# A gated second layer with seven block products for eight, in passes of three d_ff tiles and two batches

## The chip, the core and the metric

One core of a Trainium2 chip. TensorE (PE) multiplies matrices, VectorE (DVE) and ScalarE (ACT) work element by element, GpSimd (POOL) helps, SyncE (SP) issues the DMAs from one queue in order. The metric is the device time of the whole kernel in microseconds; the median of three runs before is 1274.05 us (1272.81 to 1276.3).

## The reference

Attention (4 batches, 12 heads, 448 rows, 64 columns), a feed-forward layer with squared ReLU (768 to 2048 to 768) and a gated one (768 to 1536 to 768), all in float32:

```python
q_n, k_n = rmsnorm(q, g_q), rmsnorm(k, g_k)
attn = softmax(scale * q_n @ k_n.T) @ v
x = attn.transpose(0, 2, 1, 3).reshape(B * S, H * D)     # 1792 x 768
r = np.maximum(x @ w_in, 0.0)                            # d_ff 2048
x = (r * r) @ w_out
g = x @ w_gate                                           # d_ff 1536
silu = g * (1.0 / (1.0 + np.exp(-g)))
out = (silu * (x @ w_val)) @ w_out2
```

## The kernel before

All activations lie transposed: 128 features on the partitions, the 448 rows of one batch along the free axis. So d_model is six tiles (`KD`), the second layer's d_ff twelve (`FF2`). A float32 operand is kept as two halves, `hi` (rounded to the matmul's format) and `lo` (the rest), and a product is three matmuls, hi x hi, hi x lo, lo x hi (`mm3`, the matmuls themselves at L346). ScalarE makes `hi` by a cast (L240), VectorE `lo` by a subtraction. Weights come as 64-bit words and are decoded by `chunk`: one scaling on ScalarE, one cheap row (L311) and two full rows (L315, L318) on VectorE, then the split (L333).

The two feed-forward layers run in sweeps: one batch, a range of d_ff tiles. For each tile of layer 2, `products` computes the gate (6 x 3 matmuls into a PSUM bank of `h_free`), then the value (18 matmuls), `gated` and `valued` make Sigmoid, two multiplies and the split, and `out_of` adds the tile's share to the six output sums `y` (18 matmuls), two tiles behind (`BEHIND`). Six PSUM banks hold the sums, two the products. Three batches of layer 2 are swept in two halves of six d_ff tiles (`G2`); the sums of the first half go to `y2_d` in DRAM and are read back (`Partial`, L1256, added at L1263). X tiles of a sweep are loaded and split by `load_x` (L1181 to L1184) during the sweep before.

The order of the instructions is set by a planner inside the kernel: each step is a job with a rank and with its cost on each engine that may do it; `simulate` runs them against its own clock, and whichever job has the lowest rank when an engine is free is written down next. The chip then follows that order on each engine, strictly in turn. A line in a trace is often that of a helper. In names the two numbers behind `_1_6_15` and the like are layer, sweep, tile.

Of the kernel before, what the change touches and what calls it, by code (L numbers as in the profile page):

```python
# [9 lines left out]
F32 = mybir.dt.float32  # L10
# [9 lines left out]
KD = DM // 128  # L20
# [6 lines left out]
G2 = 6  # L27
# [21 lines left out]
IO_TILES = 6  # L49
W2_SLOTS = 16  # L50
BEHIND = 2
# [28 lines left out]
def attention_two_ffn_kernel(  # L80
# [199 lines left out]
    wt, placed, free = {}, {}, []  # L280

    def load_weights(items):
# [7 lines left out]
        def chunk(key, place, c, raw_at):  # L290
# [31 lines left out]
            if c == 0:  # L322
                yield lambda: place or free
                pool, hi_tag, lo_tag = placed[key] = place or free.pop(0)
                hilo[key] = tuple(
                    pool.tile([128, DM], F32R, tag=tag, name=f"{part}_{name}{f}")
                    for part, tag in (("hi", hi_tag), ("lo", lo_tag))
                )
                parts[key] = 0
# [32 lines left out]
    def tile_at(where, shape, dtype, name):  # L362
        return where[0].tile(shape, dtype, tag=where[1], name=name)
# [28 lines left out]

    def gated(pg, where, sig):
        yield settle["P"]
        yield lambda: ea_free
        sig["at"] = ea_free.pop(0)
        t = tile_at(sig["at"], [128, S], F32, f"sig_{sig['n']}")
        yield {"A": 424}, lambda e: e.activation(out=t, in_=pg, func=ACTF.Sigmoid)  # L398
        yield {"V": 535}, lambda e: e.tensor_tensor(out=t, in0=pg, in1=t, op=ALU.mult)  # L399
        h_free.append(where)  # L400
        sig["tile"] = t

    def valued(pv, where, sig):
        yield settle["P"]
        yield lambda: s_free and "tile" in sig
        s_at = s_free.pop(0)
        s = tile_at(s_at, [128, 2, S], F32R, f"s_{sig['n']}")
        t = sig["tile"]
        yield {"V": 535}, lambda e: e.tensor_tensor(out=t, in0=pv, in1=t, op=ALU.mult)  # L409
        h_free.append(where)  # L410
        yield {"A": 467, "W": 300}, lambda e: copy(e, s[:, 0, :], t)
        yield {"W": 535, "G": 1106}, lambda e: e.tensor_tensor(
            out=s[:, 1, :], in0=t, in1=as_f32(s[:, 0, :]), op=ALU.subtract
        )
        ea_free.append(sig["at"])
        ready[sig["n"]] = s, s_at
# [573 lines left out]
    def place(slot):  # L990
        return (w1 if slot < 24 else w2), f"w{slot}", f"w{slot + 1}"
# [100 lines left out]
    M1B, F1C, F2A, F2B = range(G1, M1), range(M1, FF1), range(G2), range(G2, FF2)  # L1092
# [6 lines left out]
    order2 = [LAST - 1] + list(range(LAST - 1)) + [LAST]  # L1099
    outs = [[out[bass.ts(j, 128), bass.ts(b, S)] for j in range(KD)] for b in range(B)]  # L1100
    sweeps += [(2, b, F2A, (), None, y2_d[b]) for b in order2[:-1]]
    sweeps += [(2, order2[-1], range(FF2), F2A, None, outs[order2[-1]])]
    sweeps += [(2, b, F2B, (), y2_d[b], outs[b]) for b in order2[:-1]]
    POST = 10000
    when, steps = {}, 0
    for layer, b, fs, *_ in sweeps:
        for f in fs:
            for key in (("in", f), ("out", f)) if layer == 1 else (("g", f), ("v", f), ("o2", f)):
                when.setdefault(key, POST + steps)
            steps += layer  # L1110
# [15 lines left out]
    later += [(w, f) for f in range(FF2) for w in ("g", "v", "o2")]  # L1126
# [26 lines left out]
    w2 = ctx.enter_context(tc.tile_pool(name="w2", bufs=1, side="right", reuse_waits="tile"))  # L1153
    w3 = ctx.enter_context(tc.tile_pool(name="w3", bufs=1, side="right", reuse_waits="tile"))
    xp2 = ctx.enter_context(tc.tile_pool(name="xp2", bufs=1, side="right", reuse_waits="tile"))
    raws += [(w3, f"raw{2 + i}") for i in range(RAWS2)]
# [36 lines left out]

    def release(key):
        del wt[key]
        free.append(placed.pop(key))
# [3 lines left out]
    def products():  # L1200
        behind = []
        ys = {}
        xs = x1[LAST]
        k = POST
        for i, (layer, b, fs, last_use, partial, dst) in enumerate(sweeps):
            n = f"{layer}_{i}"
            done = None
            for f in fs:
                if f == fs[X_AT if len(fs) > 6 else 1] and i + 1 < len(sweeps):
                    nxt, done = {}, []  # L1210
                    src = (x1_d if sweeps[i + 1][0] == 1 else x2_d)[sweeps[i + 1][1]]
                    spawn(load_x(src, n, x_tiles(n, i % 2 == 0, nxt), done, k), k)
                name = f"{n}_{f}"
                if i == 0 and f < 3:
                    release(("in", f))
                elif layer == 1:
# [41 lines left out]
    def written(ps, sums, j, n, dst):  # L1258
# [5 lines left out]
        else:  # L1264
# [3 lines left out]
            yield {"A": 424}, lambda e: e.copy(y, ps)  # L1268
        yield from dma(lambda e: e.dma_start(out=dst, in_=y), 128 * S * 4)
        io_free.append(at)  # L1270
# [3 lines left out]
    def out_of(name, n, layer, f, first, last, release_it, ys, sums, dst, k):  # L1274
        key = ("out" if layer == 1 else "o2", f)
        yield lambda: key in wt and name in ready
        w = wt[key]
# [4 lines left out]
        for j in OUT_ORDER:  # L1282
            yield from mm3(ys[j], w[0], w[1], bass.ts(j, 128), s[:, 0, :], s[:, 1, :], first, last)
            if last:
                spawn(written(ys[j], sums, j, n, dst[j]), k - 2)
        s_free.append(where)
        if release_it:
            release(key)

    spawn(products(), 0)  # L1290
    simulate(lambda: finished and not timers and not any(queues.values()))

# [80 lines left out]
```

## Time and profile before

| | |
|---|---|
| median of three runs | 1274.05 us |
| the profiled execution: span, first to last instruction | 1269.9 us |
| rest of the median around the span | 4.15 us |
| TensorE busy | 1250.5 us, 6642 matmuls |
| VectorE busy | 681.6 us, 1454 instructions |
| ScalarE busy | 563.6 us, 1259 instructions |
| GpSimd busy | 158.7 us |
| DMA | 151 MB, 119 GB/s in the mean |
| layer 2 (gate, value and output matmuls) | 733 to 1266 us |

The profile gives the span of the profiled execution; a time of its own around that span is not shown, so the 4.15 us are taken from the median. A group row of the trace reads: line, engine, operation, out<-in, sizes, count | busy us, mean ns of one | idle time of the engine just before, and who ended it. Matmuls overlap, so the duration of one (366 ns) is longer than the distance between two.

### The profile page before, as it was taken

Reading aid. Unit: us, or ns where it says so; the run is one execution under the profiler, and the core shown is the slowest. Engines: PE = TensorE matmul, PEld = TensorE weight load, DVE = VectorE, ACT = ScalarE, POOL = GpSimd, SP = SyncE. Lnnn points to the kernel's source line nnn. Section 1 sums busy time; section 2 is a strip of 40 time slices with the busy share of each in tenths; the row PEclk is TensorE's granted clock in tenths of the full one; section 3 lists DMA queues with packets and bytes.
Section 4 is the critical chain, followed back from the end, with each engine's and each line's share of the span. In section 5 each row is a group of like instructions: output and inputs, shape, how many; then the busy total and the mean of one; then the engine's idle time right before and its main releaser. Section 6 shows DMA issues by size and latency. Waiting matters only on the chain.

```text
span 1269.9 us, 18473 instructions
## 1 busy us (share of the span) xinstructions
PE 1250.5 (98%) x6642; PEld 1073.4 (85%) x6642; DVE 681.6 (54%) x1454; ACT 563.6 (44%) x1259; POOL 158.7 (13%) x275
## 2 busy tenths in 40 slices
PE   8989999999999999999999999999999999999998
PEld 6656667777778998999999999999999999999998
DVE  7999985665543996459233982212159612113122
ACT  6999876776764665236122541212036311211010
POOL 5454454343200000000000000000000000000000
PEclk9999999999999999999999999999999999999999
DMA  7576664343112666436234671201037300203021
GB/s 222 170 208 179 202 189 144 108 129 123 52 65 98 227 199 218 130 123 193 74 122 131 212 250 49 86 2 44 1 101 231 123 1 1 87 1 131 1 87 44
DMA packets 87309, 151.01 MB, mean 119 GB/s; under 512 B 16481, under 2 KB 66802, under 8 KB 87218
## 3 DMA queue, kind: packets, MB, share of 16 engines
q1 hardware_dynamic: 87218, 149.84, 37.1%
q8 instruction: 52, 0.85, 0.3%
q14 instruction: 39, 0.32, 0.1%
HBM read 120.75 MB, written 29.04 MB: 118 GB/s over the span
## 4 chain that ended last, share of the span: by engine, by line
PE 79%; DVE 11%; ACT 5%; DMA 3%; issue 2%; SPq 1%; POOL 0%; DVEq 0%; ACTq 0%
PE y L346 24%; PE h_v L346 14%; PE h_g L346 14%; PE h L346 9%; PE ya L346 4%; PE h_a L346 4%; PE o L938 3%; PE sc L767 3%; PE pt L898 2%; DVE sc L795 2%; ACT ring L809 2%; ACT turned_p L240 1%; DVE ring L833 1%; DVE wt_in L318 1%; DMA raw_in<-in_w_in_dram 1%
## 5 line engine op out<-in xcount | busy, mean ns | idle before, releaser
L346 PE MATMUL h_v<-x,hi_v 128*128 128x448 f32 x576 | 164.4, 366 | 0.0
L346 PE MATMUL h_g<-x,hi_g 128*128 128x448 f32 x576 | 164.4, 366 | 0.0
L346 PE MATMUL y<-s,hi_o 128*128 128x448 f32 x576 | 164.1, 366 | 0.0
L346 PE MATMUL y<-s,hi_out 128*128 128x448 f32 x552 | 157.3, 366 | 0.9 <-ACT ys L1268 0.9
L346 PE MATMUL h<-x,hi_in 128*128 128x448 f32 x516 | 147.2, 366 | 0.0
L399 DVE TENSOR_TENSOR sig<-h_g,sig 128x448 f32<-128x448 f32 x48 | 30.0, 624 | 215.1 <-ACT sig L398 215.0
L809 ACT ACTIVATE ring<-sc,m,rms 128x448 f32<-128x448 f32 x168 | 124.2, 746 | 14.4 <-DVE m L796 5.4
L398 ACT ACTIVATE sig<-h_g 128x448 f32<-128x448 f32 x48 | 26.1, 545 | 221.8 <-PE h_g L346 221.8
L346 PEld LDWEIGHTS h_v<-x,hi_v 128*128 128x128 f32 x576 | 108.1, 188 | 9.3
L346 PEld LDWEIGHTS h_g<-x,hi_g 128*128 128x128 f32 x576 | 108.2, 188 | 9.2
L346 PEld LDWEIGHTS y<-s,hi_o 128*128 128x128 f32 x576 | 108.1, 188 | 9.3
L346 PEld LDWEIGHTS y<-s,hi_out 128*128 128x128 f32 x552 | 103.4, 188 | 10.2 <-ACT ys L1268 1.7
L346 PE MATMUL h_v<-x,lo_v 128*128 128x448 f32 x288 | 105.4, 366 | 0.0
L346 PE MATMUL y<-s,lo_o 128*128 128x448 f32 x288 | 105.4, 366 | 0.0
L346 PE MATMUL h_g<-x,lo_g 128*128 128x448 f32 x288 | 105.4, 366 | 0.0
L346 PEld LDWEIGHTS h<-x,hi_in 128*128 128x128 f32 x516 | 96.8, 188 | 8.4
L795 DVE TENSOR_REDUCE sc<-sc 128x2 f32<-128x896 f32 (+1 forms) x96 | 93.8, 977 | 15.9 <-PE sc L767 14.4
L346 PE MATMUL y<-s,lo_out 128*128 128x448 f32 x276 | 100.8, 365 | 0.0
L240 ACT COPY turned_p<-pt 128x384 f32<-128x384 f32 (+2 forms) x167 | 88.4, 541 | 23.1 <-PE pt L898 22.1
L346 PE MATMUL h<-x,lo_in 128*128 128x448 f32 x258 | 94.4, 366 | 0.0
L240 ACT CAST s<-sig 128x448 fp32r<-128x448 f32 x48 | 27.2, 566 | 131.9 <-DVE sig L409 131.8
L938 PE MATMUL o<-turned_p,v 128*64 128x448 f32 x384 | 79.5, 546 | 0.6 <-DVE turned_p L242 0.5
(160 smaller groups left out, 2236.1 us busy)
## 6 DMA issues: line engine op xcount, KB each, us to landing
raw_in<-in_w_in_dram SPq DMA_DIRECT2D x32, 384.0 KB
raw_out<-in_w_out_dram SPq DMA_DIRECT2D x32, 384.0 KB
kq<-in_kq_p_dram SPq DMA_DIRECT2D x23, 480.0 KB
xr<-x2d SPq DMA_DIRECT2D x42, 224.0 KB
raw_g<-in_w_gate_dram SPq DMA_DIRECT2D x24, 384.0 KB
raw_v<-in_w_val_dram SPq DMA_DIRECT2D x24, 384.0 KB
raw_o<-in_w_out_dram SPq DMA_DIRECT2D x24, 384.0 KB
xr<-x1d SPq DMA_DIRECT2D x36, 224.0 KB
```

The lines of the kernel that those rows point to most:

```text
L240: e.copy(out, src)
L318: yield {"W": 469}, lambda e: e.scalar_tensor_tensor(out=ti, in0=ai, scalar=3, in1=ti, op0=ALU.logical_shift_left, op1=ALU.bitwise_or)
L346: return {"P": 203}, lambda e: e.matmul(ps, lhsT=w, rhs=x, start=first, stop=last), 0
L398: yield {"A": 424}, lambda e: e.activation(out=t, in_=pg, func=ACTF.Sigmoid)
L399: yield {"V": 535}, lambda e: e.tensor_tensor(out=t, in0=pg, in1=t, op=ALU.mult)
L767: e.matmul(parts[t][:, :S], lhsT=q[a][d, bass.ts(i % 4, 128)], rhs=k[c][d], start=(p == 0), stop=(p == len(passes) - 1),)
L795: e.tensor_reduce(out=top, in_=sc, axis=AX.X, op=ALU.max, negate=True)
L809: yield {"A": 704}, lambda e: e.activation(out=slot(i), in_=parts[t][:, :S], func=ACTF.Exp, bias=m[:, t:t + 1], scale=rq[:, i:i + 1], accu ...
L833: yield {"V": 130, "G": 260}, lambda e: e.tensor_copy(dst, slot(i)[:, 384:])
L898: e.transpose(ps[:, bass.ts(j + (i > 3), 128)], p[:, bass.ts(j, 128)], ident)
L938: e.matmul(o[64 * h:64 * h + 64], lhsT=v[:, 4 * h + j], rhs=turned_p[:, 4 * h + j if j < 3 else 3], start=(j == 0), stop=(j == 3),)
```

## The change

Layer 2 is computed for a pair of batches at a time, `PAIRS` (2, 0) and (1, 3). The d_model axis is cut in two halves of three tiles. For a d_ff tile the weights form a 2 x 2 block matrix, `a11` and `a12` the two halves of the gate, `a21` and `a22` those of the value; the X tiles form another, `b11`, `b21` the halves of the first batch, `b12`, `b22` those of the second. The 2 x 2 product of blocks takes seven block products (Strassen's algorithm, in Winograd's form) of 3 x 3 matmuls instead of eight. For it four sums of weight blocks (`s1` to `s4`) and four of X blocks (`t1` to `t4`) are formed in float32 on VectorE and split into halves, and the products `p1` to `p7` are added up from PSUM on VectorE (`u2`, `u4`, `g1` and so on) into gate and value of both batches. Silu is one ScalarE operation in place of Sigmoid and a multiply.

Passes: a group of three d_ff tiles for one pair, then for the other pair; the next group starts with the pair just used, so that X changes between passes 0 and 1, 2 and 3, 4 and 5, 6 and 7. A unit is one d_ff tile of one pass (63 matmuls). After the three units of a pass come its twelve output sums (`outputs`, 108 matmuls): four begin with the first two tiles and are ended when the third is ready, the other eight follow whole. The sums of a pass go to `y2_d`, and from the pair's second pass on those of the pass before are read back and added. All eight PSUM banks serve products and sums in turn. In the built program 6363 matmuls become 6147.

The weights of layer 2 are loaded by `load_second`, from the time on when all of layer 1's are loaded; their ranks begin at six below those of their first unit, those of X at two below. Eight tiles `io` (two of them lent to the products' sums) serve X loads, partial sums and results.

```diff
-G2 = 6
-IO_TILES = 6
+IO_TILES = 7
+PAIRS = ((2, 0), (1, 3))
+GROUP = 3
+PARTIALS = 4
+SPARES = 2
...
+            if i == len(sweeps) - 2:
+                x_free.extend([(xp2, f"x{j}") for j in range(4)] + [(xp, "x6"), (xp, "x7")])
+                spawn(load_pair(0), k)
...
+        yield from second_layer(k)
...
+    def gate_value(f, slots, parts, done, temps, rank):
...
+        yield lambda: "a22" in done
+        yield from halved("a22", "a22")
+        yield lambda: "a21" in done
+        yield put("a22", "a21", "a22", ALU.add)
+        yield lambda: "a11" in done
+        yield put("a21", "a11", "a21", ALU.subtract)
+        second = []
+        spawn(last_halved("s1", "a22", lambda: second), rank)
+        spawn(last_halved("s3", "a21"), rank)
+        yield from halved("a11", "a11")
+        yield put("a11", "a22", "a11", ALU.subtract)
...
+    def load_pair(n):
...
+        rank = POST + steps + sum(2 * len(fs) for _, fs in passes[:n]) - 2
...
+        for kk in range(3):
+            parts, done, slots = {}, set(), []
+            for name, h, j in (("b11", 0, kk), ("b12", 1, kk), ("b22", 1, kk + 3), ("b21", 0, kk + 3)):
+                yield lambda: io_free
+                at = io_free.pop(0)
+                parts[name] = tile_at(at, [128, S], F32, f"{name}_{n}_{kk}"), at
+                spawn(fetched(parts[name][0], pair[h], j, name, done), rank)
+            spawn(pair_tiles(n, kk, X, slots, parts, done, rank), rank)
...
+        b1, b1_at = yield from bank_tile(f"p1_{n}_{f}")
+        yield from product(b1, "a11", "b11", True, True)
+        b6, b6_at = yield from bank_tile(f"p6_{n}_{f}")
+        got = {}
+        spawn(gate_0(got, b1, b1_at, f"{n}_{f}"), k)
+        yield from product(b6, "s2", "t2", True, True)
+        spawn(sum_2(got, b6, b6_at, f"{n}_{f}"), k)
...
+        b4, b4_at = yield from bank_tile(f"p4_{n}_{f}")
+        yield from product(b4, "a22", "t4", True, True)
+        spawn(value_0(got, b4, b4_at, (n, f, 0)), k)
...
+    def silu(t):
+        return {"A": 467}, lambda e: e.activation(out=t, in_=t, func=ACTF.Silu)
...
+    def value_0(got, ps, where, key):
+        yield settle["P"]
+        yield lambda: "u3" in got
+        u2 = got["u2"][0]
+        yield plus(u2, ps, u2)
+        h_free.append(where)
+        yield from gated(got, "g0", "u2", key)
+
+    def gated(got, gate, value, key):
+        yield lambda: gate in got
+        (g, g_at), (t, t_at) = got[gate], got[value]
+        yield {"W": 535, "G": 1106}, lambda e: e.tensor_tensor(out=t, in0=g, in1=t, op=ALU.mult)
+        ea_free.append(g_at)
+        yield lambda: s_free
+        at = s_free.pop(0)
+        s = tile_at(at, [128, 2, S], F32R, "s_%d_%d_%d" % key)
+        yield from halves_of(s, t, S)
...
+        for j, h in y_order[:ahead]:
+            ys[j, h] = yield from bank_tile(f"y2_{n}_{j}_{h}")
+            yield from chain(j, h, fs[:-1])
+        for m, (j, h) in enumerate(y_order):
+            if m >= ahead:
+                ys[j, h] = yield from bank_tile(f"y2_{n}_{j}_{h}")
+            yield from chain(j, h, fs[-1:] if m < ahead else fs)
+            spawn(summed_out(n, p, j, h, ys[j, h], sums), k)
```

The first place is VectorE at the end of layer 1's last sweep, before: the rows that end with the low half of tile 15's squares, `s_1_6_15` (`wt_v5`, `lo_g5` and the like are weights of layer 2, `r` the relu).

```order
L315 SCALAR_TENSOR_TENSOR wt_v5_0_8261<-wa_v5_0_8252,wt_v5_0_8261 128x384
L311 TENSOR_SCALAR wt_g5_1_8257<-raw_g5_1_8180 128x384
L318 SCALAR_TENSOR_TENSOR wt_v5_0_8261<-wa_v5_0_8252,wt_v5_0_8261 128x384
L333 TENSOR_TENSOR lo_g5_8274<-wt_g5_0_8210,hi_g5_8273 128x384
L315 SCALAR_TENSOR_TENSOR wt_g5_1_8257<-wa_g5_1_8242,wt_g5_1_8257 128x384
L333 TENSOR_TENSOR lo_v5_8293<-wt_v5_0_8261,hi_v5_8292 128x384
L383 SCALAR_TENSOR_TENSOR r_1_6_15_8284<-h_1_6_15_8240,r_1_6_15_8284 128x448
L311 TENSOR_SCALAR wt_v5_1_8298<-raw_v5_1_8220 128x384
L387 TENSOR_TENSOR s_1_6_15_8283<-r_1_6_15_8284,s_1_6_15_8283 128x448
```

The same place now, up to the same subtraction (`a12_2`, `s2_2`, `s4_2` and `o0` are operands of layer 2's weights, `t4_0_2` one of the first pass's X):

```order
L1293 TENSOR_TENSOR a12_2_8187<-a12_2_8077,a12_2_8187 128x384
L1315 TENSOR_SCALAR o0_0_plain_8178<-raw_o0_0_8179 128x384
L1293 TENSOR_TENSOR t4_0_2_8197<-b21_0_2_8069,t4_0_2_8197 128x448
L1298 TENSOR_TENSOR a12_2_8077<-a12_2_8077,a11_2_7967 128x384
L1318 SCALAR_TENSOR_TENSOR o0_0_plain_8178<-raw_o0_0_8179,o0_0_plain_8178 128x384
L1315 TENSOR_SCALAR o0_1_plain_8189<-raw_o0_1_8190 128x384
L1321 SCALAR_TENSOR_TENSOR o0_0_plain_8178<-raw_o0_0_8179,o0_0_plain_8178 128x384
L1293 TENSOR_TENSOR s4_2_8205<-a12_2_8077,s4_2_8205 128x384
L1318 SCALAR_TENSOR_TENSOR o0_1_plain_8189<-raw_o0_1_8190,o0_1_plain_8189 128x384
L1293 TENSOR_TENSOR o0_0_8211<-o0_0_plain_8178,o0_0_8211 128x384
L1321 SCALAR_TENSOR_TENSOR o0_1_plain_8189<-raw_o0_1_8190,o0_1_plain_8189 128x384
L393 TENSOR_TENSOR s_1_6_15_8089<-r_1_6_15_8090,s_1_6_15_8089 128x448
```

Before, one row stands between relu and subtraction of tile 15; now there are thirteen, all of them layer 2's operands, and more of these lie ahead of the relu.

The second place is VectorE at the end of the third pass (number 2), from the first sum with `p7` of the last unit to the low half of that unit's value, `s_2_5_0` (`u2`, `u4` are sums on the way to the values; `t2_3_0`, `t3_3_0`, `b21_3_0`, `t4_3_0` operands of the next pass's X):

```order
L1533 TENSOR_TENSOR u2_2_5_9730<-p7_2_5_9772,u2_2_5_9730 128x448
L1293 TENSOR_TENSOR t2_3_0_9785<-b22_3_0_9683,t2_3_0_9785 128x448
L1293 TENSOR_TENSOR t3_3_0_9786<-b12_3_0_9682,t3_3_0_9786 128x448
L1533 TENSOR_TENSOR u4_2_5_9760<-p7_2_5_9772,u4_2_5_9760 128x448
L1293 TENSOR_TENSOR b21_3_0_9787<-b21_3_0_9684,b21_3_0_9787 128x448
L1533 TENSOR_TENSOR u2_2_5_9730<-p4_2_5_9792,u2_2_5_9730 128x448
L1601 TENSOR_TENSOR u4_2_5_9760<-g1_2_5_9775,u4_2_5_9760 128x448
L1298 TENSOR_TENSOR b21_3_0_9684<-b21_3_0_9684,b22_3_0_9683 128x448
L1601 TENSOR_TENSOR u2_2_5_9730<-u1_2_5_9711,u2_2_5_9730 128x448
L1293 TENSOR_TENSOR s_2_5_1_9830<-u4_2_5_9760,s_2_5_1_9830 128x448
L1293 TENSOR_TENSOR t4_3_0_9835<-b21_3_0_9684,t4_3_0_9835 128x448
L1293 TENSOR_TENSOR s_2_5_0_9843<-u2_2_5_9730,s_2_5_0_9843 128x448
```

Five of the twelve rows prepare X of the next pass; before, a value's rows stood between weights or alone.

## Rows read from the trace of the kernel before

**Rows 1.** The page: busy time, share of the span and instructions of each engine.
```profile
PE 1250.5 (98%) x6642; PEld 1073.4 (85%) x6642; DVE 681.6 (54%) x1454; ACT 563.6 (44%) x1259; POOL 158.7 (13%) x275
```
**Rows 2.** Windows: us, busy us (x instructions) of each engine, PEclk, DMA share, GB/s.
```profile
core 0: us, PE busy (x) PEld busy (x) DVE busy (x) ACT busy (x) POOL busy (x), PEclk, DMA share, GB/s
10.00:12.00 2.00, 1.86 (x25) 1.79 (x26) 1.93 (x5) 0.09 (x1) 0.93 (x1) 1.00 0.88 239
...
406.00:450.00 44.00, 44.00 (x218) 40.66 (x217) 42.29 (x95) 28.71 (x60) 0.00 (x0) 1.00 0.62 202
733.00:1266.00 533.00, 533.00 (x2615) 490.47 (x2613) 184.25 (x353) 118.36 (x231) 0.00 (x0) 1.00 0.21 71
...
1150.00:1154.00 4.00, 4.00 (x21) 3.70 (x20) 0.98 (x2) 1.54 (x3) 0.00 (x0) 1.00 0.99 323
...
1266.00:1270.00 4.00, 0.20 (x1) 0.00 (x0) 0.86 (x2) 0.00 (x0) 0.00 (x0) 0.88 0.61 225
```
**Rows 3.** Chain of waits that ended last: start, us, engine, tile, line, matmuls.
```profile
880.84 3.65 PE y L346 x18
...
1251.51 3.69 PE h_v L346 x18
```
**Rows 4.** Who waited for whom: us in total, times, longest.
```profile
ACT sig L398 <- PE h_g L346: 221.8, 42, 6.2
...
DVE sig L409 <- PE h_v L346: 90.4, 40, 2.5
```
**Rows 5.** Groups of the page: gate and value matmuls of layer 2.
```profile
L346 PE MATMUL h_v<-x,hi_v 128*128 128x448 f32 x576 | 164.4, 366 | 0.0
L346 PE MATMUL h_g<-x,hi_g 128*128 128x448 f32 x576 | 164.4, 366 | 0.0
...
L346 PE MATMUL h_v<-x,lo_v 128*128 128x448 f32 x288 | 105.4, 366 | 0.0
...
L346 PE MATMUL h_g<-x,lo_g 128*128 128x448 f32 x288 | 105.4, 366 | 0.0
```
**Rows 6.** Timeline of VectorE, 721 to 726 us: start, us, engine, line, operation.
```profile
722.00 1.16 DVE L1184 TENSOR_TENSOR x<-xr,x 128x448 fp32r<-128x448 f32 x2
723.07 0.63 DVE L387 TENSOR_TENSOR s<-r,s 128x448 fp32r<-128x448 f32 x1
...
724.54 0.56 DVE L315 SCALAR_TENSOR_TENSOR wt_g<-wa_g,wt_g 128x384 int32<-128x384 int32 x1
725.01 0.37 DVE L311 TENSOR_SCALAR wt_v<-raw_v 128x384 int32<-128x384 uint32 x1
725.28 0.56 DVE L318 SCALAR_TENSOR_TENSOR wt_g<-wa_g,wt_g 128x384 int32<-128x384 int32 x1
```
**Rows 7.** Groups of VectorE from 400 us on, shapes kept apart.
```profile
L1184 DVE TENSOR_TENSOR x<-xr,x 128x448 fp32r<-128x448 f32 x78 | 47.1, 624 | 13.2 <-ACT x L240 12.8
...
L315 DVE SCALAR_TENSOR_TENSOR wt_g<-wa_g,wt_g 128x384 int32<-128x384 int32 x24 | 13.4, 560 | 0.1
...
L311 DVE TENSOR_SCALAR wt_g<-raw_g 128x384 int32<-128x384 uint32 x24 | 8.6, 362 | 1.1 <-DMA raw_g<-in_w_gate_dram 1.1
```
**Rows 8.** Timeline, 890 to 894 us: a value's multiply, cast and subtraction.
```profile
891.87 0.62 DVE L409 TENSOR_TENSOR sig<-h_v,sig 128x448 f32<-128x448 f32 x1 [2.45 <-PE h_v L346]
...
892.53 0.57 ACT L240 CAST s<-sig 128x448 fp32r<-128x448 f32 x1 [3.77 <-DVE sig L409]
...
893.13 0.63 DVE L412 TENSOR_TENSOR s<-sig,s 128x448 fp32r<-128x448 f32 x1 [0.63 <-ACT s L240]
```
**Rows 9.** Groups of ScalarE from 400 us on.
```profile
L398 ACT ACT_TABLE_LOAD x1 | 1.3, 1283 | 0.0
```
**Rows 10.** Timeline of TensorE, 8 to 12 us.
```profile
10.14 0.99 PE L592 MATMUL rk<-rkr,pick 128*64 128x128 f32 x16 [1.07 <-ACT rkr L636]
```
**Rows 11.** Timeline of the end: the last sums and stores.
```profile
1263.20 3.66 DVE L1263 TENSOR_TENSOR yp<-y,yp 128x448 f32<-128x448 f32 x6 [6.08 <-PE y L346]
...
1263.86 3.37 SPq L1269 DMA_DIRECT2D out_dram<-yp  x6
```

More of the change, by code (lines that the diff above doesn't have):

```diff
@@ L1107, in attention_two_ffn_kernel @@
         for f in fs:
-            for key in (("in", f), ("out", f)) if layer == 1 else (("g", f), ("v", f), ("o2", f)):
+            for key in (("in", f), ("out", f)):
                 when.setdefault(key, POST + steps)
-            steps += layer
+            steps += 1
     def gains():
@@ L1272, in written, with out_of @@
             sums.load()
[L1274 to L1277, printed above, removed]
+    def out_of(name, n, f, first, last, release_it, ys, sums, dst, k):
+        yield lambda: ("out", f) in wt and name in ready
+        w = wt["out", f]
         s, where = ready.pop(name)
@@ new lines, in attention_two_ffn_kernel, with halves_of @@
+    LAST_1 = len(sweeps) - 1
+    swept = {b: next(i for i, sw in reversed(list(enumerate(sweeps))) if sw[1] == b) for b in range(B)}
+    operand, pair_x = {}, {}
+    when2 = {f: POST + steps + sum(2 * len(fs) for _, fs in passes[:i]) + 2 * passes[i][1].index(f)
+             for f in range(FF2) for i in [next(i for i, (_, fs) in enumerate(passes) if f in fs)]}
+    def halves_of(t, plain, c):
+        yield {"A": 413 if c == WC else 467, "W": 269 if c == WC else 300}, lambda e: copy(e, t[:, 0], plain)
+        yield {"W": 469 if c == WC else 535, "G": 956 if c == WC else 1106}, lambda e: e.tensor_tensor(
+            out=t[:, 1], in0=plain, in1=as_f32(t[:, 0]), op=ALU.subtract
+        )
@@ new lines, in load_pair, with fetched @@
+    def load_pair(n):
+        pair = PAIRS[passes[n][0]]
+        X = pair_x[n] = {}
+        rank = POST + steps + sum(2 * len(fs) for _, fs in passes[:n]) - 2
+        yield lambda: all((f"1_{swept[b]}", j) in stored_at for b in pair for j in range(KD))
+        def fetched(t, b, j, name, done):
+            yield from dma(lambda e: e.dma_start(out=t, in_=x2_d[b][j]), 128 * S * 4)
+            done.add(name)
+        for kk in range(3):
[6 more added lines that the diff above has]
+            spawn(pair_tiles(n, kk, X, slots, parts, done, rank), rank)
+            for _ in range(7):
+                yield lambda: x_free
+                slots.append(x_free.pop(0))
@@ new lines, in second_layer @@
+    def second_layer(k):
+        x_of = 0
+        summed_before = set()
+        for n, (p, fs) in enumerate(passes):
+            if n and passes[n - 1][0] != p:
+                x_of = n
+            last_x = n + 1 == len(passes) or passes[n + 1][0] != p
+            last_w = n % 2 == 1
+            sums = {"used": 0}
+            for f in fs:
+                if f == fs[-1]:
+                    if last_x and n + 1 < len(passes):
+                        spawn(load_pair(n + 1), k)
+                    if p in summed_before:
+                        spawn(partials(n, p, sums, k), k)
+                yield from unit(n, f, x_of, last_x and f == fs[-1], last_w, k)
+                k += 2
+            yield from outputs(n, p, fs, sums if p in summed_before else None, last_w, k)
+            summed_before.add(p)
@@ new lines, in partials, with part @@
+    def partials(n, p, sums, k):
+        def part(j, h, at):
+            y = tile_at(at, [128, S], F32, f"yp_{n}_{j}_{h}")
+            src = y2_d[PAIRS[p][h]][j]
+            yield from dma(lambda e: e.dma_start(out=y, in_=src), 128 * S * 4)
+            sums[j, h] = y, at
+        for m, (j, h) in enumerate(y_order):
+            yield lambda: io_free and m - sums["used"] < PARTIALS and (p, j, h) in y_stored
+            spawn(part(j, h, io_free.pop(0)), k)
+    y_order = [(j, h) for j in range(KD) for h in range(2)]
@@ new lines, in summed_out @@
+    def summed_out(n, p, j, h, bank, sums):
+        ps, where = bank
+        b = PAIRS[p][h]
+        last = all(q != p for q, _ in passes[n + 1:])
+        dst = outs[b][j] if last else y2_d[b][j]
+        yield settle["P"]
+        if sums is not None:
+            yield lambda: (j, h) in sums
+            y, at = sums[j, h]
+            yield {"V": 535}, lambda e: e.tensor_tensor(out=y, in0=ps, in1=y, op=ALU.add)
+            sums["used"] += 1
+        else:
+            yield lambda: io_free
+            at = io_free.pop(0)
+            y = tile_at(at, [128, S], F32, f"yw_{n}_{j}_{h}")
+            yield {"A": 424}, lambda e: e.copy(y, ps)
+        h_free.append(where)
+        yield from dma(lambda e: e.dma_start(out=dst, in_=y), 128 * S * 4)
+        y_stored.add((p, j, h))
+        io_free.append(at)
```

322 lines of the change are left out of this document (270 added, 52 removed).

## The prediction

> **What bounds the kernel now.** I read the busy times first. TensorE works 1250.5 of 1269.9 us, VectorE 681.6 [rows 1]. The windows by stage then show that the second layer, 733 to 1266 us, is TensorE without a gap: 533 of 533 us busy at granted clock 1.00, which is the upper level, 2.4 GHz, while VectorE works 184 us and the DMA engines 21% of the time [rows 2]. The chain of waits says the same. There it is one product after the other, each of 18 matmuls, and from the start of the one at 880.84 to the end of the one at 1251.51 lie 374.36 us [rows 3], which are 102 such products: 3.670 us each, 0.2039 us a matmul. Nothing but fewer matmuls shortens this stretch as long as the other engines keep up, and they do: VectorE waits 90.4 us for value products and ScalarE 221.8 us for gate products [rows 4]. Speed does not depend on how busy VectorE is either: from 406 to 450 us it is busy 42.3 of 44 us and TensorE still puts 218 matmuls into 44.0 us [rows 2].
>
> **What the change takes away.** Gate and value are 576 + 288 matmuls each, 1728 together [rows 5]. Now there are 24 units (12 d_ff tiles, 2 pairs of batches) of 7 products with 9 matmuls, 1512. The 864 of the output stay. 216 x 0.2039 = **44.0 us** less on TensorE; layer 1 and attention keep their matmuls.
>
> **What it adds on VectorE.** Counted in the order from the first eviction of layer 2 on: 467 rows of 448 columns, 228 of 384, and 56 of the cheap decode step. What one costs when rows queue up is the distance of starts, not the duration: 0.535 us (722.00 to 723.07 for two), 0.47 (724.54 to 725.01) and 0.27 (725.01 to 725.28) [rows 6], while one alone lasts 0.624, 0.560 and 0.362 [rows 7]. The sum is 467 x 0.535 + 228 x 0.469 + 56 x 0.269 = 372 us against 2376 x 0.2039 = 484 us of matmuls: 77%. At full durations it would be 291 + 128 + 20 = 439 us, 91%. So VectorE becomes busy but not the bound on average; what matters is where it is late. The X operands of a pair (21 split tiles, 12 differences) are prepared five times, and six of the eight passes read and write partial sums. POOL gets too little of it to count. ScalarE's added casts and copies are each shorter than the VectorE row that they feed (0.57 against 0.63 us for a value's cast and subtraction [rows 8]); Silu stands for Sigmoid with one less multiply, after one table load as before (1.3 us, [rows 9]), hidden under products.
>
> **Where layer 1 meets layer 2.** This is the one place where I find a wait that can't be hidden. In the last sweep of layer 1 the preparation for the first pass is ranked ahead of the last tile's squares. From r_1_6_13 to the subtraction s_1_6_15 there are now 66 VectorE rows (35 of 448, 25 of 384, 6 cheap): 35 x 0.535 + 25 x 0.469 + 6 x 0.269 = 32.1 us; before there were 35 rows, 16.0 us. VectorE cannot begin them before product h_1_6_13 has ended. TensorE, between that end and the matmul that reads s_1_6_15's low half, has 6 products (y of 11, h 14, y of 12, h 15, y of 13, y of 14) and one matmul: 22.2 us. So it stands still for 32.1 - 22.2 = 9.9 us at least, whatever the other engines do. VectorE comes about 0.6 us late to r_1_6_13, since the sums of the sweep before are ahead of it, and once waits about 1.1 us for ScalarE's casts, which stand behind the relu and square of tile 15 in its queue; the last row's own end costs 0.1. I take **12 us**, from 10 to 16: the floor is the count above, the ceiling adds two more such waits of 2 us. What is late next there is nothing: by the time TensorE is back, the operands of the first unit stand in the same queue ahead of s_1_6_15, already done.
>
> **The clock after that gap.** Before, the level falls once, after the last matmul: from 1266 to 1270 us, with 0.20 us of matmul left, the mean is 0.88 [rows 2]. A gap of 1.07 us before 10.14 us [rows 10] did not lower it, 1.00 stands there too [rows 2]. So a gap of 12 us will meet the lower level, 1.2 GHz, and the work behind it starts there. No row shows a matmul of this kernel at that level or how long the way back takes. Bounds: nothing, and at most a stretch as long as the gap done at half speed, 6 us lost. I take **2 us**, nearer to nothing because the work behind the gap is dense. The Trainium skill ("TensorE: Matmul & The Clock Gate", Part 1: The HAM clock gate) says that TensorE returns to half clock once it has idled and has to work before it is given the full one again; the row at 1266 agrees with the first half, no row here shows the second. By that rule the term is above zero, without it the sum would be 2 us smaller.
>
> **The ends of the passes.** Four of the twelve output sums begin with two of three d_ff tiles, 24 matmuls or 4.9 us, and then need the last unit's value. Its chain is an addition, a multiply, a cast and a subtraction; in the rows the last three take 891.87 to 893.76, 1.9 us, without a queue [rows 8], so 2.5 us with the addition. But operand rows stand between. At the end of the third pass, from the sum with p7 (1.83 us before p4 ends) to the subtraction of s_2_5_0, 12 rows lie, 6.4 us; 6.4 - 1.8 + 0.1 = 4.7 against 5.1 us to the matmul that reads it. It just fits, with nothing left for a DMA that is late, and three of the rows between need tiles that were just loaded. I take 0.4 us for each of eight ends, **3 us**, from 0 to 12 (1.5 each, the length of one cast and one subtraction more).
>
> **DMA.** Layer 2 moves 18 more X loads and 54 more partial loads and stores each, 126 x 0.229 = 29 MB, to the 71 GB/s x 533 us = 38 MB of before. In the worst stretch, last unit and outputs with an X change (35 us), 12 X tiles, 12 partial loads and 12 stores are 8.3 MB, 25.6 us at the 323 GB/s of 1150 to 1154 us [rows 2]. SP's one queue holds an X load behind a store whose sum must be done first; followed row by row, the operands of the next pass are ready 2 to 4 us before TensorE wants them. I cost it at nothing, cover gone at some 3 us of lateness, 0 to 4 us in all. The tail stays: six sums and stores end 3.7 us after the last matmul [rows 2, 11]; now the last sum comes alone, at most 0.5 us less.
>
> **Sum.** -44.0 + 12 + 2 + 3 + 0 = -27 us. In the profiled execution that makes the span 1243; its span lies 4.15 us under the median of 1274.05, and I leave that part as it is: **1247 us**. Its own range is 1240 (only the counted 10 us) to 1256.
>
> **Rivals.** (a) The gap at the layer change isn't there, because the two engines drift so that VectorE enters this stretch with its preparation done. Then only the pass ends stay, -44 + 3: 1233. For it speaks that VectorE has idle time one sweep earlier; against it, that the 66 rows stand in a fixed order behind h_1_6_13.
> (b) The ends of the passes and changes of X cost 2.5 us each more, because a late load at the head of VectorE's queue holds the value chain, with 0.4 us spare: 1247 + 8 x 2.5 = 1267. For it speaks the thin margin; against it, that DMA has a quarter of its time free even there.
> (c) Slower: VectorE becomes the bound of all of layer 2. Of its rows, 261 subtract a half that ScalarE has just cast. If half of them wait 0.63 us at the head of the queue, as the one at 893.13 did [rows 8], and rows then don't overlap, 439 + 82 = 521 us stand against 484 of matmuls, +37: -44 + 37 + 14 = +7, 1281. It decides from 514 us of VectorE time on, 38% above the 372 us that I counted. For it speaks that both engines wait in order; against it that TensorE's pace leaves 60 us a pass for 45 to 54 us of VectorE rows.
> (d) The change doing less than it says can't be: the matmuls are counted in the order, 6147 against 6363.
>
> **Chances.** Forecast 0.60, (a) 0.13, (b) 0.21, (c) 0.06. The time is that of the forecast; the range, 1232 to 1268, leaves out the better part of (a), (c) and the upper part of (b), together some 2 in 10. A measurement of this kernel tells 0.3% from no change, 3.8 us. Faster than 1270.2: forecast, (a) and the greater part of (b), 0.91. Same 0.04, slower 0.05.
>
> **What would show it.** Right: TensorE's first long idle time sits before a y matmul that reads s_1_6_15, ended by VectorE, 10 to 16 us long; the granted clock falls below 1.00 there and nowhere else in layer 2; windows of one pass (60.6 us of matmuls) are 60 to 62 us long; VectorE is busy 75 to 90% of them. Wrong: no such gap (a), gaps of 2 us and more before y2 matmuls or p1 at each pass end (b), or TensorE waiting for VectorE at every p product (c).

## The result and the profile after

The kernel with seven block products takes **1246.55 us** (median of four runs, 1243.29 to 1246.79) against 1273.43 us for the kernel before on the same chip (four runs, 1272.57 to 1276.3): a ratio of 0.9776, 95% interval 0.976 to 0.9792, or 26.9 us less. The forecast was 1247.

The page of the profile after, first the span and then the busy line that answers to [rows 1]:

```profile
span 1245.0 us, 18922 instructions
...
PE 1212.4 (97%) x6426; PEld 1038.3 (83%) x6426; DVE 884.9 (71%) x1825; ACT 625.8 (50%) x1382; POOL 169.1 (14%) x285
```

TensorE has 216 records less than before, all from gate and value, and works 38.1 us less; VectorE works 203.3 us more, and its share goes from 54% to 71%. The groups of TensorE (columns as in [rows 5]; the last column is idle time before the group, and who ended it) say where TensorE stands still: nowhere within layer 2.

```profile
L352 PE MATMUL y<-s,o 128*128 128x448 f32 x864 | 177.0, 366 | 0.0
...
L352 PE MATMUL y<-s,hi_out 128*128 128x448 f32 x552 | 158.8, 369 | 13.4 <-DVE s L393 13.4
...
L352 PE MATMUL p<-t,s 128*128 128x448 f32 x648 | 144.7, 367 | 0.0
...
L352 PE MATMUL p<-b,a 128*128 128x448 f32 x432 | 96.2, 367 | 0.0
```

`p<-` are the seven products, `y<-s,o` the output sums of layer 2, where idle time at the ends of the passes would show: 0.0. `y<-s,hi_out` is layer 1, and its 13.4 us are one gap.

The windows (columns as in [rows 2]) show this gap and what follows it, and then three stretches of layer 2 of 60 us, about a pass each:

```profile
740.00:745.00 5.00, 0.00 (x0) 0.00 (x0) 5.00 (x11) 3.33 (x8) 0.00 (x0) 0.59 0.23 79
745.00:750.00 5.00, 0.00 (x0) 0.00 (x0) 5.00 (x12) 1.69 (x5) 0.00 (x0) 0.50 0.16 41
750.00:755.00 5.00, 4.65 (x14) 4.22 (x15) 3.98 (x9) 2.02 (x4) 0.00 (x0) 0.55 0.64 209
755.00:760.00 5.00, 5.00 (x26) 4.63 (x25) 1.72 (x4) 0.98 (x2) 1.01 (x1) 1.00 0.85 279
...
860.00:920.00 60.00, 60.00 (x296) 55.21 (x295) 47.07 (x93) 28.80 (x58) 1.01 (x1) 1.00 0.46 144
920.00:980.00 60.00, 60.00 (x295) 54.85 (x294) 55.29 (x107) 24.46 (x50) 1.02 (x1) 1.00 0.55 169
...
1040.00:1100.00 60.00, 60.00 (x296) 55.23 (x295) 55.73 (x108) 25.29 (x50) 1.03 (x1) 1.00 0.54 166
```

TensorE does nothing from 740 to 750 us while VectorE is busy in every one of these microseconds. The granted clock falls to 0.50 in it (the lower level, 1.2 GHz), stays low in the first 4 us of work behind it (14 matmuls in 4.65 us), and is 1.00 from 755 us on. In the three stretches TensorE is busy throughout at 1.00, as before, with VectorE at 78 to 93% beside it instead of the 35% of [rows 2].

**Where the 26.9 us come from.** The attention part takes different times in different executions, so I divide each profile at the first product of layer 1 behind it, `h_lead`. Its row (count, durations, first and last start), before and after:

```profile
L346 PE MATMUL h_lead<-x,hi_in x24: 362/365/369, 398.7 to 405.6; 128*128 128x448 f32 x24
```

```profile
L352 PE MATMUL h_lead<-x,hi_in x24: 362/365/369, 403.0 to 409.8; 128*128 128x448 f32 x24
```

From that start to the end of the span it is 1269.9 - 398.7 = 871.2 us before and 1245.0 - 403.0 = 842.0 after, 29.2 less. The parts: -44.0 for the matmuls, +13.4 for the gap, +0.2 because the matmul before a gap no longer overlaps the next (0.366 long, 0.204 apart), +2.0 for the clock: -28.4. Most of the rest is one end of a pass (+0.6, shown further down), a wait of 0.9 us with 0.2 of lost overlap that of the two profiles only the one before has (-1.1), and a tail 0.2 shorter: -29.1. The wait, in the waits view of TensorE (us in total, times, longest):

```profile
PE y L346 <- ACT ys L1268: 0.9, 1, 0.9
```

The 4.3 us that the attention part was longer in this execution take the difference of the two spans to -24.9. It is not the change's doing: in the other kernels' profiles, whose code is the same up to there, that start lies between 398.8 and 405.9. It goes with the granted clock of the first 200 us. Here are the profiles with the earliest and the latest `h_lead`, before (398.7) and the kernel with the gap filled whole (405.9):

```profile
0.00:200.00 200.00, 185.25 (x1207) 126.03 (x1208) 177.74 (x419) 168.52 (x416) 96.96 (x180) 1.00 0.63 190
```

```profile
0.00:200.00 200.00, 183.37 (x1168) 124.13 (x1169) 172.57 (x408) 165.42 (x408) 93.18 (x173) 0.97 0.63 187
```

Of the other eight, the three at 1.00 start `h_lead` by 400.0, the five at 0.97 to 0.99 at 400.0 or later. Why the clock falls there in one execution and not in another, no run shows.

### The profile page after: what moved, and what is told of

It reads as the page before. It is cut to its first block, busy times and chain, and to the rows that moved or that the text cites. A ratio compares the mean times of both kernels' runs of the same rounds, so it can differ in the third digit from the quotient of the medians.

```text
span 1245.0 us, 18922 instructions
## 1 busy us (share of the span) xinstructions
PE 1212.4 (97%) x6426; PEld 1038.3 (83%) x6426; DVE 884.9 (71%) x1825; ACT 625.8 (50%) x1382; POOL 169.1 (14%) x285
## 4 chain that ended last, share of the span: by engine, by line
PE 84%; DVE 7%; DMA 3%; ACT 3%; SPq 1%; issue 1%; DVEq 0%; ACTq 0%
PE y L352 27%; PE p L352 25%; PE h L352 12%; PE ya L352 5%; PE o L919 4%; PE h_a L352 4%; PE sc L748 3%; PE pt L879 2%; DVE sc L776 1%; ACT ring L790 1%; DMA kq<-in_kq_p_dram 1%; DMA rkb<-rkd 1%; DMA zd<-zr 1%; ACT turned_p L245 1%; DMA zb<-zd 1%
## 5 line engine op out<-in xcount | busy, mean ns | idle before, releaser
L352 PE MATMUL y<-s,o 128*128 128x448 f32 x864 | 177.0, 366 | 0.0
L352 PEld LDWEIGHTS y<-s,o 128*128 128x128 f32 x864 | 162.1, 188 | 13.5 <-DVE s L1293 0.4
L352 PE MATMUL y<-s,hi_out 128*128 128x448 f32 x552 | 158.8, 369 | 13.4 <-DVE s L393 13.4
L352 PE MATMUL p<-t,s 128*128 128x448 f32 x648 | 144.7, 367 | 0.0
L352 PEld LDWEIGHTS p<-t,s 128*128 128x128 f32 x648 | 121.7, 188 | 11.5 <-DVE yp L1660 0.3
L790 ACT ACTIVATE ring<-sc,m,rms 128x448 f32<-128x448 f32 x168 | 123.7, 742 | 13.7 <-DVE m L777 5.3
L1533 DVE TENSOR_TENSOR u<-p,u 128x448 f32<-128x448 f32 x144 | 88.5, 620 | 20.8 <-PE p L352 20.1
L352 PE MATMUL p<-b,a 128*128 128x448 f32 x432 | 96.2, 367 | 0.0
L352 PEld LDWEIGHTS p<-b,a 128*128 128x128 f32 x432 | 81.1, 188 | 7.1
L879 PE MATMUL pt<-ident,ring 128*128 128x128 f32 x432 | 71.1, 275 | 2.7 <-DVE sc L776 1.5
L352 PE MATMUL ya<-sa,hi_out 128*128 128x448 f32 x216 | 68.5, 391 | 0.0
L352 PE MATMUL h_a<-x,hi_in 128*128 128x448 f32 x216 | 67.8, 380 | 0.0
```

What stands on the lines that cost most here:

```text
L352: return {"P": 203}, lambda e: e.matmul(ps, lhsT=w, rhs=x, start=first, stop=last), 0
L790: yield {"A": 704}, lambda e: e.activation(out=slot(i), in_=parts[t][:, :S], func=ACTF.Exp, bias=m[:, t:t + 1], scale=rq[:, i:i + 1], accu ...
L879: e.transpose(ps[:, bass.ts(j + (i > 3), 128)], p[:, bass.ts(j, 128)], ident)
L1533: return {"V": 535}, lambda e: e.tensor_tensor(out=out, in0=ps, in1=b, op=ALU.add)
```

## The experiments

The theory: the fewer matmuls are the whole gain; the one loss is VectorE's queue at the change from layer 1 to layer 2, with the clock that falls in it; and the ends of the passes cost nothing, though barely. Rivals: the gain is in part the new passes or the one-op Silu; the gap has another cause than the rows ranked ahead of tile 15's squares; the clock has no part.

**The same kernel again.**

> The changed kernel itself, to have it on the same chip as the three that follow. Both theories: 1246.5 us within 0.3%, one idle time of TensorE of 13 to 14 us before the matmul that reads s_1_6_15, lower clock level behind it. If the start of layer 1 lies 2 to 4 us elsewhere than in the first profile, the attention part varies from run to run by itself.

1243.09 us (1241.84 to 1245.93), ratio 0.9753 [0.9732, 0.9775]. The gap is 13.40 us again, and from `h_lead` on it is 842.9 us. Two sets of four runs of one kernel differ by 3.5 us in their medians, as the attention part can (its end differs by 3.0 us between the two profiles, 403.0 and 400.0); a size of 2 us is better read from the trace.

**The squares of layer 1's last sweep ahead of the preparation.**

```diff
-                    spawn(squares(ps, where, name), k)
+                    spawn(squares(ps, where, name), k - SQ_AHEAD * (i == len(sweeps) - 1))
```

with `SQ_AHEAD = 8`.

> The squares of layer 1's last sweep get a rank 8 lower, so that they stand ahead of layer 2's operands; the work stays the same. From r_1_6_13 to s_1_6_15 there are then 30 VectorE rows, 15.1 us, against 22.2 us of products. Theory (the gap comes from the rank alone, and the clock falls because of the gap): gap and low clock go, 13.4 + 1.8 = 15.2 us less, but the operands for the first products come up to 2 us late: 1231 to 1234 us. Rival (VectorE has too much to do around the layer change, so the wait only moves): a gap of 8 us or more before the first p products, 1240 us or more.

1235.02 us (1232.67 to 1236.39), ratio 0.9682 [0.9658, 0.9706], 1 us above the upper end expected. TensorE's waits from 400 us on, all of them:

```profile
PE p L353 <- DVE t L1294: 2.0, 1, 2.0
PE p L353 <- DVE yp L1661: 1.5, 1, 1.5
PE y L353 <- DVE s L1294: 1.3, 2, 1.1
PE y L353 <- ACT s L246: 0.5, 1, 0.5
```

The 13.4 us are gone with the work unchanged, so the order on VectorE made the gap. What was pushed back is now late itself: `t`, an X operand of the first pass, by 2.0 us, and 3.3 us more turn up later in layer 2. One pair of these waits, 0.48 and 1.08 us with a lone matmul between, also brings the lower clock (0.50 from 787 to 789 us):

```profile
785.44 18.65 PE L353 MATMUL y<-s,o 128*128 128x448 f32 x83 [1.08 <-DVE s L1294]
```

At 0.2039 us each these 83 matmuls would take 17.08, so 1.6 us more are lost.

**Layer 2's weights later.** Instead of moving the squares up, the ranks of layer 2's weights begin three below their first unit, not six:

```diff
-                rank = when2[f] - W_AHEAD
+                rank = when2[f] - W2_AHEAD
...
-                    spawn(load_out(f, c, slot, t, t_at, temps, raws.pop(0)), when2[f] - W_AHEAD + 4)
+                    spawn(load_out(f, c, slot, t, t_at, temps, raws.pop(0)), when2[f] - W2_AHEAD + 4)
```

> Layer 2's weights are ranked 3 instead of 6 steps ahead of their unit; X and squares keep their ranks. 30 VectorE rows, 16.0 us, lie between r_1_6_13 and s_1_6_15. Theory: no gap, clock at 1.00 through layer 2, 1231 us (1229 to 1233). Rival (VectorE has too much to do there): weights now come late for the units of the first pass, gaps of several us before p products of tiles 1 and 2, 1238 us or more.

**1229.07 us** (1228.71 to 1230.02), ratio 0.9642 [0.9624, 0.9659]: at the lower end of what was expected, and the fastest version here, 45.5 us under the kernel before and 14.0 under the changed one in the same comparison. TensorE's waits from 400 us on, and windows at the layer change:

```profile
PE y L353 <- DVE s L1294: 0.7, 1, 0.7
PE y L353 <- ACT s L246: 0.2, 1, 0.2
```

```profile
720.00:730.00 10.00, 10.00 (x51) 9.27 (x50) 10.00 (x20) 6.56 (x14) 0.00 (x0) 1.00 0.54 150
730.00:735.00 5.00, 5.00 (x27) 4.63 (x26) 5.00 (x11) 1.51 (x3) 0.00 (x0) 1.00 0.14 43
735.00:740.00 5.00, 5.00 (x26) 4.63 (x25) 2.84 (x6) 1.61 (x3) 0.00 (x0) 1.00 0.78 265
```

VectorE still has its rush until 735 us, but what TensorE needs is no longer behind it. From `h_lead` (399.5) to the end (1226.9) it is 827.4 us, 43.8 less than before: the 44.0 of the fewer matmuls, whole. (Both stretches hold 0.9 us of waits.)

**Work for TensorE in the gap, twice.** To see the clock apart from the gap, TensorE is given transposes of the identity whose result nobody reads, just ahead of tile 15's output products; first 78, then 122:

```diff
-        for gen in behind:
+        for n, gen in enumerate(behind):
+            if n == len(behind) - 1:
+                yield lambda: h_free
+                where = h_free.pop(0)
+                ps = tile_at(where, [128, S], F32, "keep")
+                for _ in range(KEEP):
+                    yield {"P": 160}, lambda e: e.transpose(ps[:, :128], ident, ident), 0
+                h_free.append(where)
```

(The second has 108 for the planner's 160.)

> 78 transposes of a 128 x 128 tile, some 12.7 us, are put on TensorE just before the products of tile 15, where it idles; they compute nothing that is used, and VectorE's rows stay as they are. It measures the price of the clock by itself. Theory: s_1_6_15 comes no earlier, the products behind it start at the same time but at full clock: 1.8 us less than the changed kernel on this chip (1 to 2.5). Rival (the slow matmuls after the gap have another cause, such as a late operand): same time as the changed kernel.

1245.83 us, ratio 0.9773 [0.9751, 0.9794]: 2.7 us above the changed kernel where 1.8 less were expected. From `h_lead` on it is 842.0 us, as much as the changed kernel. The timeline of TensorE shows that it fills too little:

```profile
734.20 8.68 PE L1227 MATMUL keep<-ident 128*128 128x128 f32 x78
...
747.95 0.74 PE L353 MATMUL y<-s,hi_out 128*128 128x448 f32 x1 [4.87 <-DVE s L394]
```

A transpose takes 0.11 us, not the 0.16 that I had planned with; 4.87 us stay idle, and the clock falls in them too (0.51 in the window from 745 to 750 us). Inconclusive on the clock's price.

> As the filled gap before, whose 78 transposes took 8.7 us and left 4.9 us of idling in which the clock still fell; now 122, 13.2 to 13.6 us. Theory (the low clock follows from idling): no window of layer 2 below 1.00, the 12 matmuls behind the gap take 2.45 instead of 4.2 us; 1241.3 us where the changed kernel took 1243.1 on that chip (1240.5 to 1242.5), and the wait for s_1_6_15 no shorter as a whole. Rival (something else slows the matmuls behind the gap): the 12 matmuls take over 4 us again.

1243.64 us (1241.96 to 1247.49), ratio 0.9775 [0.9755, 0.9795], above the range expected. The time by itself says nothing on 2 us, since the attention part of its profile ran long (`h_lead` at 405.9). The timeline and the windows do:

```profile
739.55 13.48 PE L1227 MATMUL keep<-ident 128*128 128x128 f32 x122
752.79 0.99 PE L353 MATMUL y<-s,hi_out 128*128 128x448 f32 x2
753.62 0.37 PE L353 MATMUL y<-s,lo_out 128*128 128x448 f32 x1
753.82 0.57 PE L353 MATMUL y<-s,hi_out 128*128 128x448 f32 x2
```

```profile
745.00:750.00 5.00, 5.00 (x48) 5.00 (x47) 5.00 (x11) 2.77 (x6) 0.00 (x0) 1.00 0.02 5
750.00:755.00 5.00, 4.93 (x37) 4.54 (x36) 4.79 (x12) 1.77 (x4) 0.00 (x0) 1.00 0.52 132
```

No idle time, clock 1.00 throughout, and the matmuls from 753.62 us on are 0.2 us apart. From `h_lead` on it is 839.8 us, 2.2 and 3.1 less than in the two profiles of the changed kernel. That is the clock's price, to some 0.5 us, while VectorE's lateness is untouched: `s_1_6_15` starts 346.7 us behind `h_lead` in both kernels.

**Eight products in the same passes.** Same groups of three d_ff tiles, same pairs, ranks and one-op Silu, but eight plain block products and none of the sums of weights and X:

```diff
-                for name, w, c in (("a21", "v", 0), ("a22", "v", 1), ("a11", "g", 0), ("a12", "g", 1)):
+                for name, w, c in (("a11", "g", 0), ("a12", "g", 1), ("a21", "v", 0), ("a22", "v", 1)):
...
-                for _ in range(7):
+                for _ in range(4):
...
-        yield from halved("a22", "a22")
-        yield lambda: "a21" in done
-        yield put("a22", "a21", "a22", ALU.add)
...
+        for of in ("a11", "a12", "a21", "a22"):
+            yield lambda of=of: of in done
+            yield from last_halved(of, of)
```

> Passes of three d_ff tiles and two batches, Silu in one operation and the ranks stay; the seven block products become the eight plain ones (four sums of 18 matmuls a unit), without the sums of weight and X blocks and with 8 split tiles for 14. Matmuls are again 6363. Theory (the gain is the 216 matmuls, the passes by themselves bring and cost nothing): no gap at the layer change, since only 28 VectorE rows (13.6 us) lie before s_1_6_15; the version without a gap took 1229.1 us, 44.0 us more are 1273 us (1271 to 1276), as before the change. Rival (part of the gain comes from the new passes or from Silu): 1268 us or less.

1273.11 us (ten runs, 1270.97 to 1277.57), ratio 1.0001 [0.9988, 1.0013]. From 400 us on TensorE never waits, and from `h_lead` on it is 870.2 us against 871.2. Passes and Silu without the seven products bring and cost nothing clear of the noise, and 1 us by the trace.

**The kernel before with one-op Silu only.**

```diff
-        yield {"A": 424}, lambda e: e.activation(out=t, in_=pg, func=ACTF.Sigmoid)
-        yield {"V": 535}, lambda e: e.tensor_tensor(out=t, in0=pg, in1=t, op=ALU.mult)
+        yield {"A": 424}, lambda e: e.activation(out=t, in_=pg, func=ACTF.Silu)
```

> The kernel before with nothing changed but Silu in one operation for Sigmoid and a multiply: 48 VectorE rows less (30 us of busy time). Theory (VectorE has room before the change, TensorE bounds): same time, within 0.3%. Rival (some of the gain is Silu's): 3 us or more less.

1273.03 us (ten runs), ratio 1.0005 [0.9993, 1.0016]: one VectorE row less per gate, off the path.

**The changed kernel with Sigmoid and a second multiply.** Sigmoid and the multiplies now stand at the end of the value chain, so that the chain from the last product of a unit to its low half is one ScalarE and one VectorE operation longer:

```diff
-        return {"A": 467}, lambda e: e.activation(out=t, in_=t, func=ACTF.Silu)
+        return {"A": 467}, lambda e: e.activation(out=t, in_=t, func=ACTF.Sigmoid)
...
         yield {"W": 535, "G": 1106}, lambda e: e.tensor_tensor(out=t, in0=g, in1=t, op=ALU.mult)
+        yield silu(g)
+        yield {"W": 535, "G": 1106}, lambda e: e.tensor_tensor(out=t, in0=g, in1=t, op=ALU.mult)
```

> The changed kernel with Sigmoid and a second multiply in place of Silu: a value is multiplied by the gate, the gate becomes its Sigmoid in place, the value is multiplied again. Per unit 2 VectorE rows more (48 in all, 26 us), and the chain at a pass's end is a ScalarE and a VectorE operation longer, 1.2 us. Theory (the chain at the pass ends has under 1 us to spare, as counted): besides the gap at the layer change, gaps of 1.6 to 3.3 us before the y matmuls of a pass's third tile at seven pass ends, together 15 to 20 us: 1258 to 1266 us. Rival (the measured 0.0 us at the pass ends means room of several us): at most 1250 us.

1267.34 us (1265.96 to 1268.91), ratio 0.9957 [0.9942, 0.9972], 1.3 us above the range expected and some 24 above the changed kernel in its second set (which ran on another chip). TensorE's waits:

```profile
PE y L352 <- DVE s L393: 13.4, 1, 13.4
PE y L352 <- ACT s L245: 7.3, 7, 1.7
PE y L352 <- DVE s L1293: 6.4, 7, 1.4
```

Seven of the eight pass ends now wait twice, once for the cast and once for the subtraction, 13.7 us, where I had expected 15 to 20 in all. From `h_lead` on it is 866.5 us, 23.6 over the changed kernel's second profile; waits make 14.4 of that (with one of 0.7 before a product). The rest is in the timeline and the windows of the pass ends, here of one at 1118 us and one at 992:

```profile
1117.93 0.47 PE L352 MATMUL y<-s,o 128*128 128x448 f32 x1 [1.33 <-ACT s L245]
1119.83 18.93 PE L352 MATMUL y<-s,o 128*128 128x448 f32 x83 [1.42 <-DVE s L1293]
...
992.41 17.41 PE L352 MATMUL y<-s,o 128*128 128x448 f32 x83 [1.43 <-DVE s L1293]
```

```profile
1118.00:1120.00 2.00, 0.58 (x2) 0.29 (x3) 2.00 (x5) 0.66 (x2) 0.00 (x0) 1.00 0.63 248
1120.00:1122.00 2.00, 2.00 (x7) 1.80 (x8) 2.00 (x6) 1.22 (x3) 0.00 (x0) 0.60 0.00 0
1122.00:1124.00 2.00, 2.00 (x7) 1.77 (x7) 2.00 (x5) 0.00 (x0) 0.00 (x0) 0.55 0.53 146
...
992.00:994.00 2.00, 1.59 (x8) 1.47 (x9) 2.00 (x6) 1.15 (x3) 0.00 (x0) 1.00 0.00 0
```

Behind two gaps of 1.33 and 1.42 us with one matmul between them the clock falls, and 83 matmuls take 18.93 us where 83 x 0.2039 + 0.16 = 17.08 would do. The seven such rows are 18.92, 18.93, 17.09, 17.41, 17.09, 18.93 and 17.41 us long, 6.2 us over seven times 17.08. The three of 18.92 and 18.93 ran into the lower clock; the two of 17.41 did not (1.00 behind 992.41), and no run shows what their 0.3 us each are. That makes 20.6; each of 14 gaps also takes away an overlap of neighbouring matmuls, 0.16 us or, after the lone matmul of 0.47 us, 0.27: 3.0 us. Sum 23.6.

## Why the prediction was right, step by step

**What bounds it, and the 44.0 us.** Right. With the gap taken out by weights that come later, the stretch from `h_lead` on is 43.8 us shorter than before, and eight products in the same passes give no gain. TensorE stays the bound with VectorE at up to 93% in a window; I had said 75 to 90%. The passes take 60.6 to 61.2 us, where I had said 60 to 62.

**The gap at the layer change: the mechanism was right and the size off, 13.4 for 12.** The timeline of VectorE has the term that was too small:

```profile
713.27 0.62 DVE L1298 TENSOR_TENSOR b<-b,b 128x448 f32<-128x448 f32 x1
715.25 0.56 DVE L1293 TENSOR_TENSOR a<-a,a 128x384 fp32r<-128x384 f32 x1 [1.35 <-ACT a L245]
...
717.19 0.62 DVE L389 SCALAR_TENSOR_TENSOR r<-h,r 128x448 f32<-128x448 f32 x1
...
726.95 1.25 DVE L1321 SCALAR_TENSOR_TENSOR a<-raw_a,a 128x384 int32<-128x384 int32 x1
...
749.66 0.64 DVE L393 TENSOR_TENSOR s<-r,s 128x448 fp32r<-128x448 f32 x1
```

The row at 717.19 is the relu square of tile 13 (`r_1_6_13`), the one at 749.66 is `s_1_6_15`, and TensorE's matmul that reads it starts at 750.35:

```profile
736.59 0.36 PE L352 MATMUL y<-s,hi_out 128*128 128x448 f32 x1
750.35 0.74 PE L352 MATMUL y<-s,hi_out 128*128 128x448 f32 x1 [13.40 <-DVE s L393]
...
755.80 1.99 PE L352 MATMUL p<-b,a 128*128 128x448 f32 x9
```

From 717.19 to 749.66 are 32.47 us. Of the 66 rows counted, 32.1 us, all but the last one's 0.535 lie there: 31.6, so 0.9 us more than counted, where I had put 1.1 for a wait for ScalarE's casts. The size fits by luck: the waits view lists no wait of VectorE in this stretch, which is busy for 32.40 us of it. 0.7 of the 0.9 are the row at 726.95, 1.25 us long where its like take 0.56; it runs beside the one row that GpSimd has in this stretch (726.63, 1.16 us), and whether that is the cause is not shown. From the last row's start to the matmul it is 0.69 us against 0.635 counted. The product `h_1_6_13` ends at 714.87 (its last matmul starts at 714.50 and lasts 0.37), and from there TensorE had work for 22.1 us, as counted. But `r_1_6_13` starts 2.3 us behind that end, not 0.6. These 1.7 us are the miss, and 1.35 of them are a wait. At 713.89 VectorE was through with its rows, and then it waited 1.35 us at the head of its queue for a cast that ScalarE began only at 714.70:

```profile
714.70 0.51 ACT L245 CAST a<-a 128x384 fp32r<-128x384 f32 x1 [4.86 <-PE h L352]
```

That cast itself waited 4.86 us for the product: in the code the place of a weight of layer 1 is released when its last product is written down, and layer 2's operand `a` goes to such a place. So the end of `h_1_6_13` held up the cast, the cast held up a subtraction of layer 2, and behind it, after three more rows, stood the relu square of the same product. The chain is read from the trace and the code; no run took it away by itself, and the other 0.35 us are not traced. I had followed the rows on one queue, not the buffer that they go into.

**The clock, +2: right in place and size.** The 17 matmuls from 750.35 us to the first product at 755.80 take 5.45 us, 17 x 0.2039 = 3.47, so 2.0 us. The size had been chosen between bounds of 0 and 6, so that it fits is in part luck. The kernel with the gap filled gains 2 to 3 us by the clock alone. The rule that I cited from the Trainium skill ("TensorE: Matmul & The Clock Gate", Part 1: The HAM clock gate) has both its halves in these rows now: the level falls in the idle time and comes back only behind some work.

**The ends of the passes, +3: 0.6 in fact.** At the end of pass 1, the first row of TensorE and the rows of VectorE; the two rows from 976 us on, one of them a weight load (PEld), are from the end of pass 3:

```profile
855.05 22.05 PE L352 MATMUL y<-s,o 128*128 128x448 f32 x108
...
976.55 22.64 PE L352 MATMUL y<-s,o 128*128 128x448 f32 x108
...
981.76 17.04 PEld L352 LDWEIGHTS y<-s,o 128*128 128x128 f32 x83 [0.36 <-DVE s L1293]
```

```profile
855.42 0.62 DVE L1533 TENSOR_TENSOR u<-p,u 128x448 f32<-128x448 f32 x1
...
858.96 0.62 DVE L1293 TENSOR_TENSOR s<-u,s 128x448 fp32r<-128x448 f32 x1
```

The low half of the last value is done at 859.58, and the matmul that may need it is 24 behind the start of the sums: 855.05 + 24 x 0.2039 = 859.94. The margin of 0.4 us was what I had counted, and at seven of the eight ends it holds: their 108 matmuls take 22.04 to 22.07 us. At the end of pass 3 it does not: a weight load waits 0.36 us for the subtraction, and the sums take 22.64, 0.6 more. The idle time of TensorE hides this, since its busy time goes on. So charging 0.4 for each end, on top of a count that fitted, was the mistake; one late end is what there was (in the second profile of the same kernel two ends take 22.39 and 22.38). How thin the margin is, the kernel with Sigmoid shows: one link more in this chain costs 24 us in all, about what rival (b) would have cost.

**DMA, +0: right.** At 46 to 55% DMA share in the three stretches shown, no matmul waits for a load. **The tail**, at most 0.5 us less: the span now ends 3.4 us after the last matmul, against 3.7.

**The 4.15 us around the span** were left as they were, and here the forecast had luck. A run's time is mostly 1.8 us above its span (1246.79 to 1245.0). The other 2.35 go with a quick attention part in the profile of before, whose `h_lead` starts earliest of all; that they are nothing else is not shown. The forecast of -27 was too small against -29.2 in the stretch that the change touches (the gap was 1.6 larger with its overlap, the pass ends 2.4 smaller, and the 1.1 of a wait that went away and the 0.2 of the tail were not in the sum), and the start of `h_lead` moves by up to 7 us from one profile to another.

**The rivals.** (a), no gap, is false, though it is what the version with later weights makes true, at 1229. (b) is false: the ends cost 0.6 us together, not 2.5 more each. (c) is false: VectorE never bounds a pass. That Silu or the passes carry a part, which I had not listed, falls with the two kernels at 1.0001 and 1.0005.

## What to carry to other kernels

When a change gives work from the bound engine to another one, count the other engine's queue where two stages meet: the average (77% here) says nothing about it, and preparation ranked too early cost a third of the gain. Preparation for the next stage must stand behind the last rows of this one, and as late as its own first use permits: three steps ahead gave all of the 44 us, six gave 28. For each row ahead of the critical one ask also which buffer it writes and who still holds that buffer.

## What the runs showed of the hardware that I had not expected

- The granted clock falls with gaps much shorter than 13 us: with one of 4.87 us, and behind four pairs of gaps shorter than 2 us each with a lone matmul between, three of the seven in the kernel with Sigmoid (1.73 and 0.53; 1.32 and 1.43; 1.33 and 1.42) and one in that with the squares first (0.48 and 1.08), at 1.6 to 1.85 us each. Behind the pair of 1.35 and 1.43 it stayed at 1.00, so the length alone does not decide. The Trainium skill ("TensorE: Matmul & The Clock Gate", A second HAM failure mode: psum-queue depth-cycling) tells of the clock being lost to short idle times between groups of matmuls in another kernel; these rows agree.
- Transposes of 128 columns, 0.11 us each, hold the clock at 1.00 for 13.5 us as matmuls do.
- VectorE and TensorE can both be over 90% busy for 60 us without slowing each other: 295 and 296 matmuls in such windows, as in those with VectorE at 78%.
